# Linear attention with a gated convolution block: key projections in plain float32, plain float32 for the second batch's queries, and the convolution's middle tap on ScalarE

## The chip, the cores and the metric

The kernel runs on one core of a Trainium2 chip. A core has five engines that each work through their own queue in order: TensorE (matmuls; PE in the profile, its weight loads PEld), VectorE (DVE), ScalarE (ACT), GpSimd (POOL) and SyncE (SP), which issues the transfers here. The metric is the time of one execution on the device in microseconds; lower is better.

## The reference, cut to what matters

```python
def _attn_ref(q, k, v, w_phi):                 # batch 8, 8 heads, 576 tokens, head size 64
    def phi(x):
        proj = np.einsum('bhsd,df->bhsf', x, w_phi)          # 128 features
        proj = proj - np.max(np.abs(proj), axis=-1, keepdims=True)
        return np.concatenate([np.exp(proj), np.exp(-proj)], axis=-1)
    q_p, k_p = (phi(q), phi(k))
    kv = np.einsum('bhsf,bhsd->bhfd', k_p, v)
    z = np.sum(k_p, axis=2)
    num = np.einsum('bhsf,bhfd->bhsd', q_p, kv)
    den = np.einsum('bhsf,bhf->bhs', q_p, z)[..., None] + 1e-06
    return num / den

def _moe_ref(x, w_in, conv_w, w_out):          # x: (8, 576, 512), inner width 1024
    h = np.maximum(x @ w_in, 0.0)
    conv_out = conv_w[0]*h[s-1] + conv_w[1]*h[s] + conv_w[2]*h[s+1]   # per channel
    gate = 1.0 / (1.0 + np.exp(-conv_out))
    return h * gate @ w_out
```

The heads of a batch, side by side, are the rows of x. Everything is float32.

## The kernel before, in words

**Two forms of a matmul.** TensorE takes operands of type float32 (plain form) or float32r, a rounded float32. To keep precision with float32r the kernel splits an operand into a rounded part hi and the rest lo (`split`, L57 to L65: one copy at L60, L62 or L64, one subtraction at L65) and makes three matmuls, hi x hi, hi x lo, lo x hi. The expert block's matmuls (hp at L429, op at L488) all have this split form.

**Units and groups.** Each batch is two units of four heads, u = 2*b + qd, 16 in all. A unit's tokens are worked in five groups: g = 0 holds one block of 128 rows (the last 64 tokens of each head pair), g = 1 to 4 hold two blocks each. So a unit has nine blocks.

**Keys** (`k_process`, L220). A group's keys are loaded, split, and projected (`load_split` L172, `project` L185): the lhsT is 128 rows of keys, the rhs the block-diagonal weight, 256 columns, result kp in PSUM. VectorE takes the largest absolute value (L204) and subtracts it (L206), ScalarE makes both exponentials ke (L236, L237), and TensorE multiplies them with v into kv (L251, L255), always plain float32. GpSimd makes the key's split: kxh at L62, kxl at L65.

**Queries** (`q_process`, L300). Load, split or not, project to qp (L196 plain, L199 to L201 split), maximum and subtraction as before, four transposes tp (L320), both exponentials (L326), then the product with kv, nm. `NQ_F32 = 2` makes the first two units' queries plain at the projection. `NKV_F32 = 2` makes the first two units plain at nm (L348); in the later units g = 0 is plain and g = 1 to 4 are split (L356), for which the exponential qe is split by ScalarE (qh at L60) and VectorE (ql at L65), and kv itself by ScalarE (kvf at L279) and VectorE (kvh at L64, kvl at L65). Unit u's nm is interleaved by hand with the kv products of unit u + 1: `after` chains each instruction behind the last, with one kv product behind two of three split matmuls, or n behind each plain one.

**From attention to the expert block.** ScalarE copies numerator and denominator out of PSUM (L374, L379), the denominators go through small transfers (L377), VectorE adds 1e-6 and takes the reciprocal (L392, L393), four transfers spread it into rr (L397), and VectorE and ScalarE make x and its split (L405, L406, L409).

**The expert block** runs over 16 halves n of 288 tokens. `h_part` (L418) makes eight tiles hp of 12 matmuls, each evicted with a Relu by ScalarE into h (L436). The PSUM pool pm that hp and op use has two buffers. `conv_process` (L441) makes the convolution in one tile c (one buffer): the middle tap c = h * cw on GpSimd (L452), the outer taps added by VectorE (L457), one sigmoid on ScalarE over all eight channels' tiles (L461), the gate's product (L465), and the split into gh (ScalarE) and gl (VectorE). `o_part` (L478) makes four tiles op of 24 matmuls, evicted at L493 and stored. A new half's first tap can be written only when the old half's gl have read c.

**What sets the order.** The Python code runs generators under a small planner: each step has a cost in nanoseconds (`pe`), a pause (`wait`), or conditions (`until`), and the loop at the end takes an attention step or an expert step, so that both end together, with the last halves of the expert block alone. The planner's costs do not depend on the form of a matmul. The instructions then go through a scheduler that simulates their times and places them in each engine's queue by readiness and priority. Expert work starts when all four head pairs of the first batch have their x. The 16 weight tiles come as float64 words and are converted by VectorE, ScalarE and GpSimd (L92 to L120) in the first 130 us or so.

Of the kernel before, what the change touches and what calls it, by code (L numbers as in the profile page):

```python
# [11 lines left out]
AF = mybir.ActivationFunctionType  # L12
ALU = mybir.AluOpType
# [7 lines left out]
TC = 288  # L21
# [7 lines left out]
AHEAD = 300  # L29

NQ_F32 = 2
NKV_F32 = 2


@with_exitstack
def kernel(
# [13 lines left out]
    nc = tc.nc  # L50
# [6 lines left out]
    def split(src, hi, lo, eng_hi, eng_lo):  # L57

        if eng_hi is nc.scalar:
            nc.scalar.activation(out=hi, in_=src, func=AF.Copy)  # L60
        elif eng_hi is nc.gpsimd:
            nc.gpsimd.tensor_scalar(out=hi, in0=src, scalar1=1.0, scalar2=0.0, op0=ALU.mult, op1=ALU.add)  # L62
        else:
            nc.vector.tensor_copy(out=hi, in_=src)  # L64
        eng_lo.tensor_tensor(out=lo, in0=src, in1=hi.bitcast(F32), op=ALU.subtract)  # L65
# [56 lines left out]
    cw = cp.tile([P, 24], F32, name="cw")  # L122
# [7 lines left out]
    cw = cw.rearrange("p (f k) -> p f k", k=3)  # L130
# [25 lines left out]
    def wait(ns):  # L156
        return ("wait", ns * LAT)

    def until(*keys):
        return ("until", [k for k in keys if k is not None])  # L160

    def set_ready(key, ns=0):
        ready[key] = now[0] + ns * LAT
# [5 lines left out]
    def group_columns(g):  # L169
        return (512, 1) if g == 0 else ((g - 1) * 256 + (P if g > 2 else 0), 2)  # L170

    def load_split(src, b, qd, g, kind):  # L172
        c0, n = group_columns(g)
        if kind == "q" and 2 * b + qd < NQ_F32:
            raw = sb.tile([P, n * P], F32, name=f"{kind}r{b}_{qd}_{g}", tag=kind + "xh", bufs=2)
            nc.sync.dma_start(out=raw, in_=src[b, qd, :, c0 : c0 + n * P])
            return n, raw, None
        raw = sb.tile([P, n * P], F32, name=f"{kind}r{b}_{qd}_{g}", tag=kind + "r", bufs=2)
        nc.sync.dma_start(out=raw, in_=src[b, qd, :, c0 : c0 + n * P])
        hi = sb.tile([P, n * P], F32R, name=f"{kind}xh{b}_{qd}_{g}", tag=kind + "xh", bufs=2)  # L180
        lo = sb.tile([P, n * P], F32R, name=f"{kind}xl{b}_{qd}_{g}", tag=kind + "xl", bufs=2)
        split(raw, hi, lo, nc.gpsimd, nc.gpsimd)
        return n, hi, lo
# [36 lines left out]
    def k_process(b, qd, g):  # L220
# [4 lines left out]

        yield until(back("kp", 2), back("kv", 4))
        n, hi, lo = load_split(kT, b, qd, g, "k")
        v0 = 16 if g == 0 else 4 * (g - 1)
        v = sb.tile([P, 4 * VW], F32, name=f"v{b}_{qd}_{g}", tag="v", bufs=4)
# [40 lines left out]
        if g == 4:  # L270
# [4 lines left out]
            for i in range(2):  # L275
                kf = None
                if 2 * b + qd >= NKV_F32:
                    kf = sb.tile([P, 2, 2 * VW], F32, name=f"kvf{b}_{qd}_{i}", tag="kvf", bufs=2)
                    nc.scalar.activation(out=kf, in_=kp[i], func=AF.Copy)  # L279
                hi = sb.tile([P, 2, 2 * VW], F32 if 2 * b + qd < NKV_F32 else F32R, name=f"kvh{b}_{qd}_{i}", tag="kvh", bufs=4)  # L280
                if 2 * b + qd < NKV_F32:
                    nc.scalar.activation(out=hi, in_=kp[i], func=AF.Copy)
# [17 lines left out]
    def q_process(b, qd, g):  # L300
# [4 lines left out]

        yield until(back("qp", 2))
        n, hi, lo = load_split(qT, b, qd, g, "q")
        yield wait(3000)
        yield until(back("tp", 2))
# [8 lines left out]
        for t in range(n):  # L318
            for i in range(2):
                nc.tensor.transpose(out=tp[:, i, t, :], in_=pr[:, 2 * t + i, :], identity=idn)  # L320
        f32 = 2 * b + qd < NKV_F32 or g == 0
        qh = sb.tile([P, 2, 2, n * P], F32 if f32 else F32R, name=f"qh{b}_{qd}_{g}", tag="qh", bufs=2)
# [95 lines left out]
    def h_part(n):  # L418
        b, c = divmod(n, 2)
        yield until(*[("x", b, p, c) for p in range(4)], "w_in")  # L420
        spawn(conv_process(n))
        for f in range(8):
            ps = pm.tile([P, HW], F32, name=f"hp{n}_{f}", tag="m")
            k = 0
            for p in range(4):
                xa, xb = xh[b, p, c], xl[b, p, c]
                wa, wb = win_hi[p][:, f * P : (f + 1) * P], win_lo[p][:, f * P : (f + 1) * P]
                for w_, x_ in ((wa, xa), (wa, xb), (wb, xa)):
                    nc.tensor.matmul(out=ps, lhsT=w_, rhs=x_, start=(k == 0), stop=(k == 11))  # L429
                    k += 1  # L430
                if p % 2 == 1:
                    yield pe(740)
            if 8 * n + f >= NH:
                yield until(("gate", 8 * n + f - NH))
            hs = sb.tile([P, HW], F32, name=f"h{n}_{f}", tag="h", bufs=NH)
            nc.scalar.activation(out=hs, in_=ps, func=AF.Relu)  # L436
            ht[n, f] = hs
            set_ready(("hs", n, f), 500)
        set_ready(("h", n))

    def conv_process(n):  # L441
        c = n % 2
        o = 0 if c == 0 else HW - TC
        for f in range(8):
            yield until(("hs", n, f), ("g4", n - 1) if n > 0 else None)
            if f == 0:
                c4 = sb.tile([P, 8, TC], F32, name=f"c{n}", tag="c", bufs=1)
            hs = ht.pop((n, f))
            ct[n, f] = hs, c4
            cv = c4[:, f, :]  # L450

            nc.gpsimd.tensor_scalar(out=cv, in0=hs[:, o : o + TC], scalar1=cw[:, f, 1:2], scalar2=0.0,  # L452
                                    op0=ALU.mult, op1=ALU.add)
            for j in (0, 2):
                lo = 1 if (c, j) == (0, 0) else 0
                hi = TC - 1 if (c, j) == (1, 2) else TC
                nc.vector.scalar_tensor_tensor(out=cv[:, lo:hi], in0=hs[:, o + j - 1 + lo : o + j - 1 + hi],  # L457
                                               scalar=cw[:, f, j : j + 1], in1=cv[:, lo:hi],
                                               op0=ALU.mult, op1=ALU.add)
        yield wait(2000)  # L460
        nc.scalar.activation(out=c4, in_=c4, func=AF.Sigmoid)  # L461
        for f in range(8):
            set_ready(("gate", 8 * n + f))
            hs, c4 = ct[n, f]
            nc.vector.tensor_tensor(out=c4[:, f, :], in0=c4[:, f, :], in1=hs[:, o : o + TC], op=ALU.mult)  # L465
        yield wait(3000)
        yield until(("o", n - 1) if n > 0 else "w_out")
        for f in range(8):
            hs, c4 = ct.pop((n, f))
            if f % 4 == 0:  # L470
                gh4 = sb.tile([P, 4, TC], F32R, name=f"gh{n}_{f}", tag="gh", bufs=2)
                gl4 = sb.tile([P, 4, TC], F32R, name=f"gl{n}_{f}", tag="gl", bufs=2)
            gt[n, f] = gh4[:, f % 4, :], gl4[:, f % 4, :]
            split(c4[:, f, :], *gt[n, f], nc.scalar, nc.vector)
        set_ready(("g4", n))
        set_ready(("g", n), 3000)
# [81 lines left out]
    while moe is not None or chains or active:  # L558
        while chains and sum(1 for p in active if p[2]) < WINDOW:
            b, x, g, kind = chains.pop(0)  # L560
# [82 lines left out]
```

## Time and profile before

| | |
|---|---|
| median of three runs | 827.91 us |
| those runs | 826.32, 827.91, 1064.72 us |
| the profiled execution | 825.6 us, its span 823.5 us, mean granted TensorE clock 0.989 |
| instructions | 17817 |
| read from HBM, written | 38.13 MB, 9.44 MB |

The span is the time from the first profiled instruction to the last. Busy times are sums of an engine's instructions; matmuls overlap in TensorE's pipeline, so the time that one costs is read from the starts of neighbours and not from its own duration. A row of a group gives line, engine, operation, output and inputs by the program's names, shape and count, then busy time and mean duration, then the engine's idle time ahead of these instructions and what ended it.

### The profile page before, as it was taken

The numbers are of one execution on the slowest core, as the hardware profiler recorded it, in microseconds if no ns is written. First come the engines' busy times: TensorE is split into PE (matmuls) and PEld (weight loads), VectorE is DVE, ScalarE is ACT, GpSimd is POOL, SyncE is SP. The second block draws the span as 40 slices with busy tenths as digits, with TensorE's granted clock in tenths as the row PEclk, the third lists the DMA queues.
The fourth block names the chain that finished last, engine by engine and source line by source line (L and its number), as shares of the span: only waits on it lengthen the run. The fifth ranks groups of instructions, "written<-read, shape, count | busy, mean of one in ns | idle before, by whom it ended". The sixth has DMA issues, their size and how long they took to land.

```text
span 823.5 us, 17817 instructions
## 1 busy us (share of the span) xinstructions
PE 788.0 (96%) x6350; PEld 772.5 (94%) x6350; DVE 645.6 (78%) x1390; ACT 569.5 (69%) x1228; POOL 307.6 (37%) x467
## 2 busy tenths in 40 slices
PE   7778779999999999999999999999999999999998
PEld 6767678999999999999999999999999999999998
DVE  4879999799987769787779878788697878766551
ACT  4598777797788867687586857678576867644332
POOL 4757765444443424414233333424334131111110
PEclk9799989999999999999999999999999999999999
DMA  6544421211211302121121211112021100000001
GB/s 187 157 134 135 135 66 47 67 41 44 70 56 44 93 18 71 27 82 50 46 61 43 69 34 60 47 50 82 15 77 29 56 12 19 13 30 30 23 23 44
DMA packets 56328, 49.18 MB, mean 60 GB/s; under 512 B 15024, under 2 KB 54192, under 8 KB 56240
## 3 DMA queue, kind: packets, MB, share of 16 engines
q1 hardware_dynamic: 56240, 48.05, 20.1%
q8 instruction: 51, 0.84, 0.4%
q14 instruction: 37, 0.30, 0.1%
HBM read 38.13 MB, written 9.44 MB: 58 GB/s over the span
## 4 chain that ended last, share of the span: by engine, by line
PE 74%; DVE 10%; ACT 7%; issue 4%; DMA 3%; POOL 1%; SPq 1%; DVEq 0%; ACTq 0%; POOLq 0%
PE op L488 22%; PE hp L429 21%; PE kv L255 8%; PE nm L356 8%; PE tp L320 3%; PE kp L199 2%; PE nm L348 2%; PE kp L200 2%; PE kp L201 2%; PE qp L199 1%; PE qp L200 1%; PE qp L201 1%; DMA w_r<-in_w_in_dram 1%; PE kv L251 1%; DVE qm L204 1%
## 5 line engine op out<-in xcount | busy, mean ns | idle before, releaser
L457 DVE SCALAR_TENSOR_TENSOR c<-h,cw,c 128x287 f32<-128x287 f32 (+1 forms) x256 | 138.7, 554 | 49.4 <-POOL c L452 47.5
L452 POOL TENSOR_SCALAR c<-h,cw 128x288 f32<-128x288 f32 x128 | 75.0, 588 | 243.6 <-ACT h L436 184.3
L255 PE MATMUL kv<-v,ke 128*128 128x65 f32 x1024 | 159.4, 255 | 1.4 <-ACT ke L236 1.2
L255 PEld LDWEIGHTS kv<-v,ke 128*128 128x128 f32 x1024 | 153.5, 193 | 4.8 <-ACT ke L236 1.8
L429 PE MATMUL hp<-xh,win_hi 128*128 128x290 f32 x512 | 153.2, 300 | 0.6 <-ACT os L493 0.6
L429 PE MATMUL hp<-xl,win_hi 128*128 128x290 f32 x512 | 152.7, 298 | 0.2 <-DVE xl L65 0.2
L488 PE MATMUL op<-gh,wout_hi 128*128 128x288 f32 x512 | 152.2, 298 | 0.0
L429 PE MATMUL hp<-xh,win_lo 128*128 128x290 f32 x512 | 151.9, 297 | 0.0
L488 PE MATMUL op<-gl,wout_hi 128*128 128x288 f32 x512 | 151.4, 296 | 0.0
L488 PE MATMUL op<-gh,wout_lo 128*128 128x288 f32 x512 | 150.9, 295 | 0.0
L436 ACT ACTIVATE h<-hp 128x290 f32<-128x290 f32 x128 | 52.2, 414 | 71.7 <-PE hp L429 71.2
L429 PEld LDWEIGHTS hp<-xh,win_hi 128*128 128x128 f32 x512 | 96.7, 190 | 1.5 <-ACT os L493 1.4
L62 POOL TENSOR_SCALAR kxh<-kr 128x256 fp32r<-128x256 f32 (+1 forms) x80 | 43.8, 547 | 144.1 <-PE kp L200 134.6
L429 PEld LDWEIGHTS hp<-xl,win_hi 128*128 128x128 f32 x512 | 97.0, 189 | 0.6 <-DVE xl L65 0.6
L429 PEld LDWEIGHTS hp<-xh,win_lo 128*128 128x128 f32 x512 | 97.1, 190 | 0.0
L488 PEld LDWEIGHTS op<-gh,wout_lo 128*128 128x128 f32 x512 | 96.4, 188 | 0.0
L488 PEld LDWEIGHTS op<-gl,wout_hi 128*128 128x128 f32 x512 | 96.2, 188 | 0.0
L488 PEld LDWEIGHTS op<-gh,wout_hi 128*128 128x128 f32 x512 | 96.1, 188 | 0.0
L65 DVE TENSOR_TENSOR ql<-qe,qh 128x512 fp32r<-128x512 f32 x112 | 79.9, 732 | 9.9 <-ACT qh L60 9.5
L236 ACT ACTIVATE ke<-ks 128x512 f32<-128x512 f32 (+1 forms) x80 | 46.9, 586 | 39.1 <-DVE ks L206 36.5
L326 ACT ACTIVATE qe<-tp 128x512 f32<-128x512 f32 x112 | 61.2, 595 | 12.2 <-PE tp L320 10.4
L356 PE MATMUL nm<-ql,kvh 128*65 128x256 f32 x224 | 68.4, 308 | 0.3 <-DVE ql L65 0.2
(84 smaller groups left out, 1989.5 us busy)
## 6 DMA issues: line engine op xcount, KB each, us to landing
v<-in_vt_dram SPq DMA_DIRECT2D x80, 130.0 KB
out_dram<-os SPq DMA_DIRECT2D x64, 144.0 KB
qr<-in_qT_dram SPq DMA_DIRECT2D x64, 128.0 KB
kr<-in_kT_dram SPq DMA_DIRECT2D x64, 128.0 KB
w_r<-in_w_in_dram SPq DMA_DIRECT2D x8, 512.0 KB
w_r<-in_w_out_dram SPq DMA_DIRECT2D x8, 512.0 KB
rr<-rc SPq DMA_DIRECT2D x128, 2.2 KB
qr<-in_qT_dram SPq DMA_DIRECT2D x16, 64.0 KB
```

The costliest lines, as they stand in the source:

```text
L62: nc.gpsimd.tensor_scalar(out=hi, in0=src, scalar1=1.0, scalar2=0.0, op0=ALU.mult, op1=ALU.add)
L65: eng_lo.tensor_tensor(out=lo, in0=src, in1=hi.bitcast(F32), op=ALU.subtract)
L199: nc.tensor.matmul(out=o, lhsT=his, rhs=wbd_hi, start=True, stop=False)
L236: nc.scalar.activation(out=e[:, 0], in_=pr, func=AF.Exp)
L255: ins = nc.tensor.matmul(out=kp[i][:, s, p0 : p0 + VW], lhsT=lhsT, rhs=v[:, (2 * t + i) * VW : (2 * t + i + 1) * VW], start=False, stop=(g ...
L326: nc.scalar.activation(out=e, in_=tp.rearrange("p i t s -> p i (t s)"), func=AF.Exp, scale=1.0 - 2.0 * s)
L356: ins = after(ins, lambda: nc.tensor.matmul(out=ps[:, i, o : o + w], lhsT=w_, rhs=x_, start=(k == 0), stop=(k == 5)))
L429: nc.tensor.matmul(out=ps, lhsT=w_, rhs=x_, start=(k == 0), stop=(k == 11))
L436: nc.scalar.activation(out=hs, in_=ps, func=AF.Relu)
L452: nc.gpsimd.tensor_scalar(out=cv, in0=hs[:, o : o + TC], scalar1=cw[:, f, 1:2], scalar2=0.0, op0=ALU.mult, op1=ALU.add)
L457: nc.vector.scalar_tensor_tensor(out=cv[:, lo:hi], in0=hs[:, o + j - 1 + lo : o + j - 1 + hi], scalar=cw[:, f, j : j + 1], in1=cv[:, lo:hi ...
L488: nc.tensor.matmul(out=ps, lhsT=w_, rhs=x_, start=(k == 0), stop=(k == 23))
```

## The change

Three edits. The keys' tiles are loaded as float32 and go into the projection unsplit, for all 16 units (before, only queries of the first two units did); the tile uses the buffers (tag kxh, two of them) that held the rounded part, and the matmul reads it directly. `NKV_F32 = 4` takes the second batch's two units into the plain form of nm: their kv is copied out of PSUM once as float32, and the exponentials are written as float32 without a split. The middle tap becomes a ScalarE activation, a copy scaled by a value per partition.

```diff
 NQ_F32 = 2
-NKV_F32 = 2
+NKV_F32 = 4
...
     def load_split(src, b, qd, g, kind):
         c0, n = group_columns(g)
-        if kind == "q" and 2 * b + qd < NQ_F32:
+        if kind == "k" or 2 * b + qd < NQ_F32:
             raw = sb.tile([P, n * P], F32, name=f"{kind}r{b}_{qd}_{g}", tag=kind + "xh", bufs=2)
             nc.sync.dma_start(out=raw, in_=src[b, qd, :, c0 : c0 + n * P])
             return n, raw, None
...
-            nc.gpsimd.tensor_scalar(out=cv, in0=hs[:, o : o + TC], scalar1=cw[:, f, 1:2], scalar2=0.0,
-                                    op0=ALU.mult, op1=ALU.add)
+            nc.scalar.activation(out=cv, in_=hs[:, o : o + TC], func=AF.Copy, scale=cw[:, f, 1:2])
```

## The prediction

> **What bounds the kernel now.** I read the engine totals first, then a table of stages, and only then single instructions.
>
> ```profile
> PE 788.0 (96%) x6350; PEld 772.5 (94%) x6350; DVE 645.6 (78%) x1390; ACT 569.5 (69%) x1228; POOL 307.6 (37%) x467
> ```
>
> One average hides three stages, so the next view is the busy time of each engine per stage (columns: length, then PE, weight load, DVE, ACT, POOL, granted clock, DMA share, GB/s):
>
> ```profile
> 0.00:60.00 60.00, 45.69 (x293) 40.96 (x294) 41.43 (x76) 37.86 (x78) 34.68 (x47) 0.91 0.53 155
> 60.00:140.00 80.00, 64.88 (x497) 58.54 (x496) 78.45 (x147) 61.94 (x134) 56.61 (x66) 0.96 0.35 104
> 140.00:200.00 60.00, 58.48 (x491) 57.70 (x490) 52.83 (x117) 48.77 (x107) 26.98 (x39) 1.00 0.19 53
> 200.00:700.00 500.00, 499.65 (x4190) 497.52 (x4189) 403.33 (x888) 368.10 (x797) 173.13 (x284) 1.00 0.18 50
> ```
>
> From 200 to 700 us TensorE idles 0.35 us in 500: a microsecond more of TensorE work there is a microsecond more of time, and work taken off VectorE or GpSimd there is worth nothing. From 140 to 200 us it idles 1.5 us, nearly the same case. From 60 to 140 us VectorE is busy 78.45 of 80 us and TensorE idles 15.1: there VectorE sets the pace. In the first 60 us TensorE idles 14.3 us with no engine full. So the change has two prices: its TensorE work counts after 140 us, its VectorE work before.
>
> **What a plain product costs on TensorE.** The trap is in the counts. The source has one plain matmul per 128-token block (two query units of nine blocks are plain now, 18 matmuls), and the profile shows twice as many; the split form shows 144 of each of its three, as the source has them.
>
> ```profile
> L196 PE MATMUL qp<-wbd_f,qr 128*128 128x256 f32 x36 | 10.9, 436 | 9.5 <-DMA wbd_f<-in_wbd_dram 4.9 <-ACT qh L326 3.7 <-PE tp L320 0.9
> L199 PE MATMUL kp<-wbd_hi,kxh 128*128 128x256 f32 x144 | 49.0, 340 | 6.2 <-DVE ks L206 4.0 <-POOL wout_lo L65 2.0 <-ACT num L379 0.2
> L348 PE MATMUL nm<-qh,kvh 128*65 128x256 f32 x64 | 19.5, 386 | 1.6 <-ACT qh L326 1.6
> L356 PE MATMUL nm<-qh,kvh 128*65 128x256 f32 x224 | 63.1, 286 | 0.6 <-ACT qh L60 0.6
> ```
>
> So a plain float32 matmul is issued as two instructions. The mean durations (436, 340, 286 ns) overlap in the pipeline and say nothing of cost; the distance from start to start does. In TensorE's timeline:
>
> ```profile
> 15.36 1.46 PE L196 MATMUL qp<-wbd_f,qr 128*128 128x256 f32 x6
> 16.66 0.27 PE L320 MATMUL tp<-idn,qs 128*128 128x128 f32 x1
> ...
> 231.92 0.28 PE L199 MATMUL kp<-wbd_hi,kxh 128*128 128x256 f32 x1
> ...
> 232.27 0.29 PE L199 MATMUL kp<-wbd_hi,kxh 128*128 128x256 f32 x1
> ```
>
> Six plain instructions take 16.66 - 15.36 = 1.30 us, 0.217 each, so a plain block costs 0.434 us. Three split matmuls, from one L199 to the next, take 0.35 us. **Plain is 0.08 us dearer per block.** Bounds: where a split triple follows plain work, its first start-to-start is 0.20 us, not 0.12 (228.12 to 228.32 below), which would make the old form 0.43 and the difference nothing; and a lone plain block between split ones can add that same 0.08 to its successor, which makes it 0.16. As the plain rows before a switch look shortened by about as much, I take 0.08.
>
> ```profile
> 228.12 0.36 PE L199 MATMUL kp<-wbd_hi,kxh 128*128 128x256 f32 x1
> 228.32 0.28 PE L200 MATMUL kp<-wbd_lo,kxh 128*128 128x256 f32 x1
> ```
>
> The Trainium skill, page "FP8 and Floating Point Precision", section "TensorE Precision Notes", says that true float32 takes four passes through the array. Counted as four split matmuls of 0.35/3 = 0.117 us that would be an estimate of 0.47 us a block; the trace has 0.434, and its row is what I use.
>
> The second half of the change on TensorE is L348 for L356 in the second batch. A step of one projection half with its interleaved key products, plain (57.27 to 58.10: two nm, four kv instructions) and split (230.12 to 230.81: three nm and two rows of two kv between):
>
> ```profile
> 57.27 0.59 PE L348 MATMUL nm<-qh,kvh 128*65 128x256 f32 x2
> 57.70 0.56 PE L255 MATMUL kv<-v,ke 128*128 128x65 f32 x4
> 58.10 0.60 PE L348 MATMUL nm<-qh,kvh 128*65 128x256 f32 x2
> ...
> 230.12 0.31 PE L356 MATMUL nm<-qh,kvl 128*65 128x256 f32 x1
> ...
> 230.81 0.31 PE L356 MATMUL nm<-qh,kvl 128*65 128x256 f32 x1
> ```
>
> 0.83 against 0.69 us, 0.14 dearer. Two units, four groups, four steps: 32 steps, 4.5 us.
>
> **The sum by stage.** GpSimd's split of a key group, which goes, and the reach of the key work and of the expert evictions (a tile's view: ns least/median/most, first and last start):
>
> ```profile
> L65 POOL TENSOR_TENSOR kxl<-kr,kxh 128x256 fp32r<-128x256 f32 (+1 forms) x80 | 59.6, 745 | 8.4 <-PE kp L201 4.0
> L62 POOL TENSOR_SCALAR kxh<-kr 128x256 fp32r<-128x256 f32 (+1 forms) x80 | 43.8, 547 | 144.1 <-PE kp L200 134.6 <-DMA kr<-in_kT_dram 9.4
> ...
> L199 PE MATMUL kp<-wbd_hi,kxh x144: 277/362/775, 7.3 to 660.1; 128*128 128x256 f32 x144
> ...
> L436 ACT ACTIVATE h<-hp x128: 392/413/439, 128.1 to 794.7; 128x290 f32<-128x290 f32 x128
> ```
>
> The key blocks per stage are a third of the kp matmuls (same columns, kp's instructions alone), the second batch's first 32 split products with ql lie half before 140 us and half in the next stage:
>
> ```profile
> 0.00:60.00 60.00, 13.45 (x57) 10.78 (x57) 13.01 (x22) 0.91 0.53 155
> 60.00:140.00 80.00, 10.98 (x60) 8.89 (x60) 13.75 (x22) 0.96 0.35 104
> 140.00:200.00 60.00, 8.17 (x39) 6.01 (x39) 8.88 (x14) 1.00 0.19 53
> 200.00:700.00 500.00, 64.73 (x276) 45.60 (x276) 64.20 (x102) 1.00 0.18 50
> ...
> 60.00:140.00 80.00, 5.29 (x16) 2.41 (x16) 10.30 (x10) 0.96 0.35 104
> 140.00:200.00 60.00, 7.32 (x24) 3.25 (x24) 8.32 (x13) 1.00 0.19 53
> ```
>
> 200 to 700 us: 92 blocks x 0.08 = +7.4 us, nothing to hide it. 140 to 200 us: 13 x 0.08 + 16 x 0.14 = +3.3 us. 0 to 60 us: 19 blocks, +1.5 us, against GpSimd's split (0.547 + 0.745 = 1.3 us) that leaves the way of the first key groups and 14.3 us of idle: taken as 0, between -3 and +3. After 700 us no key is projected: 0.
>
> 60 to 140 us: TensorE's +3.8 us (20 x 0.08 + 16 x 0.14) falls into 15.1 us of idle. VectorE loses these (groups of this stage alone, mean ns behind the count):
>
> ```profile
> L65 DVE TENSOR_TENSOR ql<-qe,qh 128x512 fp32r<-128x512 f32 x10 | 10.6, 1070 | 0.0
> L65 DVE TENSOR_TENSOR kvl<-kvf,kvh 128x260 fp32r<-128x260 f32 x4 | 1.7, 415 | 0.0
> L64 DVE CAST kvh<-kvf 128x260 fp32r<-128x260 f32 x4 | 1.2, 289 | 0.0
> ```
>
> That is 13.5 us off a full engine. TensorE's own 64.9 + 3.8 = 68.7 us is the floor, so the stage can shrink by at most 11.3 us. It cannot get all: ql begins only at 103 us, and SP's queue, the evictions and the key waits stay. I take -4 (0 to -11).
>
> In the Trainium skill, page "SBUF — State Buffer", section "Who interferes with whom", a VectorE instruction with two SBUF inputs contends with a GpSimd one that reads SBUF. The ql row agrees, 1070 ns here beside GpSimd busy 56.6 of 80 us; taking the key splits off GpSimd would then help the front beyond the 13.5 us, but not below TensorE's floor.
>
> **The middle tap** leaves GpSimd for ScalarE. Its rows, and the nearest on ScalarE by shape:
>
> ```profile
> L452 POOL TENSOR_SCALAR c<-h,cw 128x288 f32<-128x288 f32 x128 | 75.0, 588 | 243.6 <-ACT h L436 184.3 <-DVE gl L65 50.4 <-ACT dr L374 5.7
> L60 ACT ACTIVATE gh<-c 128x288 fp32r<-128x288 f32 x128 | 45.6, 433 | 5.3 <-PE op L488 5.2
> L60 ACT ACTIVATE qh<-qe 128x512 fp32r<-128x512 f32 x112 | 65.7, 635 | 0.1
> ```
>
> 128 x 0.433 = 55 us more on ScalarE, less 16 x 0.635 = 10 for the splits of qh: 569.5 becomes 615 us. In the 500 us stage that is 368 of 500 plus some 35, still under 82%; the cover is that idle share and the two PSUM buffers of the expert matmuls. The tap itself stands right behind the eviction of h that it reads, in the same queue. I take +1 us of new TensorE stalls, bounds -1 (VectorE waits less for the tap) and +34 (the second rival). The keys' loads now go straight into the tile that the matmul reads, two buffers instead of two and two; a group's load on SP's queue then waits for the matmul two groups back, and behind it stand v, the denominators and the outputs. With 80 groups over 653 us (7.3 to 660.1), two groups are 16 us, so I take 0 (up to +3 in the crowded front).
>
> Sum: 0 - 4 + 3.3 + 7.4 + 1 = **+7.7 us on the profiled run's 825.6, about 833**; its span is 823.5 us with 2.1 around it. The runs shown have 826.3 and 827.9 besides one far out, so I round down a little for the front: **832 us**, 0.5% above the median.
>
> **Rivals.**
> *The front gives everything back.* TensorE idle in 60 to 140 us falls to nothing (-11.3) and the start loses 3: 825.6 - 14.3 + 10.7 + 1 = 823. For it: VectorE's 98%. Against: ql starts late in that stage.
> *ScalarE stands still for the old tile.* The tap writes the single buffer c, free only when VectorE has finished all eight gl of the half before.
>
> ```profile
> POOL c L452 <- DVE gl L65: 50.4, 5, 18.3
> ...
> 701.98 0.42 ACT L436 ACTIVATE h<-hp 128x290 f32<-128x290 f32 x1
> ...
> 702.85 0.51 POOL L452 TENSOR_SCALAR c<-h,cw 128x288 f32<-128x288 f32 x1 [18.30 <-DVE gl L65]
> ```
>
> On GpSimd nobody queued behind these 50.4 us. On ScalarE the evictions do, and it decides once ScalarE stands longer than the two PSUM buffers cover, 2 x 12 matmuls x 0.13 = 3.2 us. All five waits less that cover: 50.4 - 16 = +34, 866 us, slower. Against: in the longest the eviction ended at 702.40 and the tap began at 702.85, so ScalarE would have stood 0.45 us.
> *TensorE pays in full.* The front gives nothing, TensorE's added 1.5 + 3.8 us there count too, and lone plain blocks cost their neighbours 0.08 in half the cases (+5): 825.6 + 5.3 + 10.7 + 5 + 1 = 848.
> *Plain is not dearer.* The change does less than I price: at a difference of 0 per key block, 825.6 - 4 + 2.2 + 1 = 825.
>
> **Chances.** Forecast (826 to 841) 0.55; front gives all back 0.12; plain not dearer 0.12; full price 0.13; ScalarE stands still 0.08. A measurement of this kernel can tell about 2% from no change, here 811 and 844.5 us. The two cheap cases together give 825.6 - 14.3 + 2.2 + 1 = 814.5; below 811 I leave 0.06, for that with a corner of the bounds; above 844.5 lie most of the full price and of the standing ScalarE and a corner of the forecast, 0.17; within, 0.77. The range for eight in ten, 816 to 847, takes in the cheap cases and most of the full price and leaves out the standing ScalarE.
>
> **What would show it.** TensorE busy near 803 us; L196 with kp, 288 instructions at 0.217 us start to start; L348 with 128x256 at 128, L356 at 192 each; GpSimd near 129 us (307.6 less the taps' 75 and the key splits' 103); ScalarE near 615; VectorE near 631 or less. In the steady stage each batch should take 18 blocks x 0.08 = 1.4 us longer. Wrong if it takes less (plain cheaper than its rows), if TensorE shows waits on h or os in the middle (ScalarE), or if the first expert eviction (128.1 us now) doesn't come earlier (the front).

## The result, and the profile after

The changed kernel takes 834.12 us (median of four runs, 831.43 to 837.46) against 826.32 us (median of three); the ratio is 1.0095, 95% interval 1.0074 to 1.0116. It is about one per cent slower, by 7.8 us; the forecast was 832. Runs in a slower state of the chip are left out here and below (of the kernel before 1064.72 and 854.32 us, and one of 1083.95 us of the kernel that keeps GpSimd's copies). The profiled execution of the changed kernel is its fastest run, 831.43 us with a span of 829.6.

Engine totals of the changed kernel, then its busy time by stage (length, PE, weight load, DVE, ACT, POOL, granted clock, DMA share, GB/s):

```profile
PE 799.7 (96%) x6174; PEld 770.0 (93%) x6174; DVE 611.9 (74%) x1366; ACT 623.2 (75%) x1340; POOL 134.2 (16%) x179
```

```profile
0.00:60.00 60.00, 47.31 (x298) 40.13 (x298) 43.62 (x84) 39.66 (x82) 20.47 (x22) 1.00 0.55 162
60.00:140.00 80.00, 73.06 (x498) 63.56 (x497) 67.36 (x135) 62.43 (x140) 38.44 (x40) 0.96 0.35 101
140.00:200.00 60.00, 57.69 (x444) 54.96 (x444) 46.46 (x109) 50.06 (x104) 7.87 (x14) 1.00 0.17 46
200.00:700.00 500.00, 497.06 (x4011) 487.94 (x4010) 381.18 (x868) 395.95 (x858) 67.41 (x104) 1.00 0.18 50
700.00:829.60 129.60, 124.59 (x931) 123.39 (x930) 73.25 (x175) 75.06 (x160) 0.00 (x0) 1.00 0.08 26
```

The first four rows answer to the four of before. From 60 to 140 us VectorE is no longer full (67.4 us instead of 78.45) and TensorE idles 6.9 us instead of 15.1. From 200 to 700 us TensorE idles 2.9 us instead of 0.35, and ScalarE carries 28 us more. The new waits there, by TensorE's weight loads, longest first, are on evictions of op (L492) and on qh:

```profile
PEld hp L429 <- ACT os L492: 1.7, 5, 0.6
PEld op L487 <- ACT os L492: 1.0, 2, 0.8
PEld nm L356 <- ACT qh L60: 0.7, 1, 0.7
```

The groups that the prediction named, with the tap and the evictions of h as a tile's view gives them (ns least/median/most, first and last start):

```profile
L196 PE MATMUL kp<-wbd_f,kr 128*128 128x256 f32 x288 | 81.4, 390 | 3.2 <-DMA kr<-in_kT_dram 1.9 <-PE kv L255 1.3
L348 PE MATMUL nm<-qh,kvh 128*65 128x256 f32 x128 | 40.2, 398 | 3.1 <-ACT qh L326 3.0
L452 ACT ACTIVATE c<-h,cw 128x288 f32<-128x288 f32 x128 | 67.2, 537 | 2.4 <-DVE gl L65 0.2
...
L436 ACT ACTIVATE h<-hp x128: 387/413/452, 114.6 to 800.4; 128x290 f32<-128x290 f32 x128
```

288 and 128 instructions, as two per plain matmul require. The start-to-start of a plain key block shows in TensorE's timeline: two L196 from 455.30 to the next row at 455.73, 0.43 us, the forecast's 0.434.

```profile
455.30 0.59 PE L196 MATMUL kp<-wbd_f,kr 128*128 128x256 f32 x2
455.73 0.27 PE L320 MATMUL tp<-idn,qs 128*128 128x128 f32 x1
```

The period of a batch in the steady stage shows in one eviction of the numerator, L379, in two batches that lie three apart. Before, it comes at

```profile
351.52 0.77 ACT L379 ACTIVATE num<-nm 64x256 f32<-64x256 f32 x2
...
638.97 0.76 ACT L379 ACTIVATE num<-nm 64x256 f32<-64x256 f32 x2
```

and in the changed kernel at

```profile
349.56 0.76 ACT L379 ACTIVATE num<-nm 64x256 f32<-64x256 f32 x2
...
641.85 0.77 ACT L379 ACTIVATE num<-nm 64x256 f32<-64x256 f32 x2
```

so a batch takes 97.4 us instead of 95.8, 1.6 more; 1.4 was forecast.

**Reading the span as a sum.** A span is TensorE's work at full clock, plus its idle time, plus what it loses at a lower granted clock. The loss is the span times one minus the mean clock, good to a microsecond or two, since the mean covers idle time as well. Of before: idle 823.5 - 788.0 = 35.5, loss 823.5 x 0.011 = 9.1, work 788.0 - 9.1 = 778.9. Of the changed kernel: idle 829.6 - 799.7 = 29.9, loss 829.6 x 0.005 = 4.1, work 795.6. So the span's +6.1 is work +16.7, idle -5.6, clock -5.0. The clocks (core, span, clock), before first:

```profile
core 0: 823.5 us, clock 0.989
```

```profile
core 0: 829.6 us, clock 0.995
```

### The profile page after: what moved, and what is told of

Its sections match the earlier page's. It is cut to its first block, busy times and chain, and to the rows that moved or that the text cites. A ratio compares the mean times of both kernels' runs of the same rounds, so it can differ in the third digit from the quotient of the medians.

```text
span 829.6 us, 17001 instructions
## 1 busy us (share of the span) xinstructions
PE 799.7 (96%) x6174; PEld 770.0 (93%) x6174; DVE 611.9 (74%) x1366; ACT 623.2 (75%) x1340; POOL 134.2 (16%) x179
## 4 chain that ended last, share of the span: by engine, by line
PE 74%; ACT 11%; DVE 7%; DMA 4%; issue 2%; SPq 1%; DVEq 0%; ACTq 0%
PE hp L429 22%; PE op L487 19%; PE kv L255 8%; PE nm L356 7%; PE kp L196 6%; PE tp L320 3%; PE nm L348 3%; PE qp L199 1%; ACT gh L60 1%; DMA w_r<-in_w_in_dram 1%; PE qp L200 1%; PE kv L251 1%; PE qp L201 1%; ACT num L379 1%; ACT ke L237 1%
## 5 line engine op out<-in xcount | busy, mean ns | idle before, releaser
L429 PE MATMUL hp<-xh,win_hi 128*128 128x290 f32 x512 | 155.9, 306 | 3.3 <-ACT os L492 1.7
L456 DVE SCALAR_TENSOR_TENSOR c<-h,cw,c 128x287 f32<-128x287 f32 (+1 forms) x256 | 127.4, 516 | 38.3 <-ACT c L452 36.6
L62 POOL TENSOR_SCALAR qxh<-qr 128x256 fp32r<-128x256 f32 (+1 forms) x70 | 32.1, 465 | 463.8 <-PE qp L200 310.3
L487 PEld LDWEIGHTS op<-gh,wout_lo 128*128 128x128 f32 x512 | 96.4, 188 | 0.0
L65 DVE TENSOR_TENSOR ql<-qe,qh 128x512 fp32r<-128x512 f32 x96 | 67.4, 712 | 23.3 <-ACT qh L60 22.8
L196 PE MATMUL kp<-wbd_f,kr 128*128 128x256 f32 x288 | 81.4, 390 | 3.2 <-DMA kr<-in_kT_dram 1.9
L326 ACT ACTIVATE qe<-tp 128x512 f32<-128x512 f32 x96 | 53.6, 597 | 25.3 <-PE tp L320 24.5
L65 DVE TENSOR_TENSOR gl<-c,gh 128x288 fp32r<-128x288 f32 x128 | 55.0, 480 | 21.8 <-ACT gh L60 21.7
L452 ACT ACTIVATE c<-h,cw 128x288 f32<-128x288 f32 x128 | 67.2, 537 | 2.4 <-DVE gl L65 0.2
```

What stands on the lines that cost most here:

```text
L196: nc.tensor.matmul(out=o, lhsT=his, rhs=wbd_f, start=True, stop=True)
L326: nc.scalar.activation(out=e, in_=tp.rearrange("p i t s -> p i (t s)"), func=AF.Exp, scale=1.0 - 2.0 * s)
L452: nc.scalar.activation(out=cv, in_=hs[:, o : o + TC], func=AF.Copy, scale=cw[:, f, 1:2])
```

## The experiments

The theory: plain matmuls add TensorE work that counts after 140 us, and the front is set by VectorE. Its rivals: GpSimd's copies set the front, the tap on ScalarE makes the loss, or the order of the queues does. The first eight kernels are the three edits alone, in pairs, and two versions with plain keys in four units; all twelve kernels stand in one table behind them, split as above. The kernel before, timed again beside them, had medians of 825.6 to 825.9 us; the ratios are against these.

**Keys alone.**

```diff
-        if kind == "q" and 2 * b + qd < NQ_F32:
+        if kind == "k" or 2 * b + qd < NQ_F32:
```

> Only the keys are projected in plain float32; nm and the middle tap are as before. Theory A (TensorE's added work counts after 140 us, the front is set by VectorE): 105 blocks after 140 us at 0.08 us give +8.4 us, the front gains little because VectorE keeps its work, so +6 to +9 us against before (833 to 836); first expert eviction near 126 us. Rival B (GpSimd's reads slow VectorE in the front): taking the key splits off GpSimd frees the front, first expert eviction near 118 us, TensorE idle before 140 us down from 29.4 to about 22, and the total only about +1 us. Rival C (the tap on ScalarE is what costs): keys alone about 0.

845.68 us, ratio 1.0234 (1.0212 to 1.0256): more than twice the loss of the whole change, which no theory expected. First eviction at 121.5 us, between the two. TensorE's work is near its price (+12.8 us), the rest is idle time (+7.6): four batches have a stall of 2.4 or 3.4 us. TensorE's timeline at one of them, then ScalarE's:

```profile
353.99 0.63 PE L348 MATMUL nm<-qh,kvf 128*65 128x64 f32 x8
358.00 0.33 PE L356 MATMUL nm<-qh,kvh 128*65 128x256 f32 x1 [3.37 <-ACT qh L60]
...
359.47 0.44 PE L488 MATMUL op<-gl,wout_hi 128*128 128x288 f32 x1
359.71 0.44 PE L488 MATMUL op<-gh,wout_lo 128*128 128x288 f32 x1
```

```profile
350.69 2.13 ACT L461 ACTIVATE c<-c 128x2304 f32<-128x2304 f32 x1
...
353.44 1.28 ACT L236 ACT_TABLE_LOAD   x1
354.74 0.63 ACT L236 ACTIVATE ke<-ks 128x512 f32<-128x512 f32 x1
355.28 0.61 ACT L237 ACTIVATE ke<-ks 128x512 f32<-128x512 f32 x1
355.91 0.59 ACT L374 ACTIVATE dr<-nm 1x512 f32<-1x512 f32 x1
356.52 0.76 ACT L379 ACTIVATE num<-nm 64x256 f32<-64x256 f32 x2
357.31 1.15 ACT L60 ACTIVATE qh<-qe 128x512 fp32r<-128x512 f32 x2
```

TensorE stands 3.37 us for qh, and ScalarE is never idle in it: qh stands behind the sigmoid, a table load, another group's exponentials and an eviction. The bracket says who ended the wait; the second fence says why so late. Afterwards the expert matmuls start 0.24 us apart, not 0.13.

**nm alone.**

```diff
-NKV_F32 = 2
+NKV_F32 = 4
```

> Only the second batch's nm is plain; keys stay split, the tap stays on GpSimd. Theory A: VectorE loses 13.5 us in the front, first expert eviction 6 to 10 us earlier than 128, TensorE idle before 140 us down by 4 to 8 us; 16 steps after 140 us at 0.14 us give +2.2 us; total -2 to -6 us. Rival B (front relief comes from GpSimd): eviction stays near 128 us and the total is +2 to +4 us.

826.45 us, ratio 1.0011 (0.9999 to 1.0024), no change. The eviction comes at 122.2 us and the work grows by 3.2, as expected; the total misses the expected gain, because idle and clock together give back only 2.4.

**Tap alone.**

```diff
-            nc.gpsimd.tensor_scalar(out=cv, in0=hs[:, o : o + TC], scalar1=cw[:, f, 1:2], scalar2=0.0,
-                                    op0=ALU.mult, op1=ALU.add)
+            nc.scalar.activation(out=cv, in_=hs[:, o : o + TC], func=AF.Copy, scale=cw[:, f, 1:2])
```

> Only the middle tap moves to ScalarE. Theory A: ScalarE about 625 us busy, TensorE gets waits on os and h in the middle, some 2 to 4 us of idle after 140 us, total +1 to +4 us. Rival C (ScalarE is what costs): +6 us or more, with most of the change's loss in it. If the tap costs nothing at all, 0 within 1 us, and the 2.6 us of new idle after 200 us must come from another edit.

827.72 us, ratio 1.0024 (1.0015 to 1.0034), +2 us. It is not what costs.

**The pairs**: keys and nm (the tap put back), keys and tap (nm put back), nm and tap (the keys put back). The edits are the ones above.

```diff
-            nc.scalar.activation(out=cv, in_=hs[:, o : o + TC], func=AF.Copy, scale=cw[:, f, 1:2])
+            nc.gpsimd.tensor_scalar(out=cv, in0=hs[:, o : o + TC], scalar1=cw[:, f, 1:2], scalar2=0.0,
+                                    op0=ALU.mult, op1=ALU.add)
```

> The change with the tap put back on GpSimd. Theory A: the tap's share of the loss goes, 830 to 833 us, and TensorE's waits on os in the middle with it. Rival C: back to 826 or less. No matter which, GpSimd is busy 75 us more than with the whole change.

848.06 us, ratio 1.0259 (1.0240 to 1.0278): without the tap's edit the change is slower by 14 us more. A miss for every theory.

```diff
-NKV_F32 = 4
+NKV_F32 = 2
```

> The change without plain nm. Theory A: VectorE keeps 13.5 us of work in the front, first expert eviction later than the whole change's 114.6 us by 5 us or more, total 836 to 840 us. Rival B: eviction still near 118 us, total within 2 us of the whole change's 834.

834.27 us, ratio 1.0092 (1.0069 to 1.0115), the whole change's time; the eviction comes at 122.0 us, later as theory A says, but the total is below its range and is the one that rival B gave.

```diff
-        if kind == "k" or 2 * b + qd < NQ_F32:
+        if kind == "q" and 2 * b + qd < NQ_F32:
```

> The change without plain keys. Theory A: no key cost after 140 us (8.4 us), the front still relieved on VectorE: 822 to 828 us, the period per batch back at 95.9 us from 97.4. Rival (the period grows because of ScalarE's extra work, not because of the keys): the period stays near 97 us and the total near 834.

826.91 us, ratio 1.0010 (0.9998 to 1.0022): without plain keys the loss is gone. The loss needs the keys; how large it is depends on the tap.

**Plain keys in the first four units only**, with plain nm, and the tap on either engine.

```diff
-        if kind == "q" and 2 * b + qd < NQ_F32:
+        if 2 * b + qd < (4 if kind == "k" else NQ_F32):
```

> Keys are plain only in the first two batches' units (four of 16), nm is plain in the second batch, the tap stays on GpSimd. This keeps the front's relief and drops the key cost after 200 us (92 blocks, 7.4 us) and the tap. Theory A: 826 - 8 (front idle) + 3.3 (140 to 200 us) or a little more of TensorE work, 819 to 824 us, below both kernels. Rival B expects the same, since GpSimd is relieved too. Rival C expects 826. If plain keys are not dearer after 200 us, this is no better than all keys plain with nm.

827.31 us, ratio 1.0015 (1.0000 to 1.0030). A miss: work +7.2 against -5.8 of idle and clock. The front's relief is paid for by the work that buys it.

> Plain keys in the first four units alone, plain nm in the second batch, tap on ScalarE. Against the same kernel with the tap on GpSimd this prices the tap once more: Theory A +1 to +4 us, 821 to 827 us; period 95.9 us per batch as the keys after 200 us are split. If the tap relieves VectorE (shared reads with GpSimd) more than it loads ScalarE, it is 1 to 2 us faster instead.

829.36 us, ratio 1.0045 (1.0029 to 1.0061), above its range; against the same kernel with the tap on GpSimd it is 2 us more, as theory A has it.

**Plain keys in another order.** With the tap on ScalarE the stall is rare: none over 1.2 us behind 140 us in the changed kernel, one of 1.76 us on qh in that with keys and tap. In the changed kernel ScalarE's queue has the exponentials of that query group and qh together, behind the evictions; with the keys alone qe stands ahead of the sigmoid and qh some 14 us behind qe. To have that order without the tap, only a priority is changed.

```diff
-            nc.scalar.activation(out=e, in_=tp.rearrange("p i t s -> p i (t s)"), func=AF.Exp, scale=1.0 - 2.0 * s)
-            if not f32:
-                split(e, qh[:, s], ql[:, s], nc.scalar, nc.vector)
+            with tc.high_priority(offset=600):
+                nc.scalar.activation(out=e, in_=tp.rearrange("p i t s -> p i (t s)"), func=AF.Exp, scale=1.0 - 2.0 * s)
+                if not f32:
+                    split(e, qh[:, s], ql[:, s], nc.scalar, nc.vector)
```

> Plain keys, tap on GpSimd, as in the kernel with the keys alone (843.2 us span, a stall of 2.4 or 3.4 us in nearly every batch while TensorE waits for qh behind a sigmoid and two table loads on ScalarE). The only edit besides: the queries' exponentials and their split get a higher priority of 600, which changes the order in ScalarE's queue and no instruction. Theory D (those stalls come from the queue order that the scheduler made, not from plain keys as such): the stalls go, the period per batch falls from 101.1 to about 97.4 us and the total to 831 to 836 us, as with the tap on ScalarE. Rival E (with the tap on GpSimd, plain keys stall TensorE in any order): it stays at 840 to 848 us.

826.96 us, ratio 1.0013 (1.0004 to 1.0022): 18.7 us less than with the keys alone, without one instruction less on TensorE, and below the range of either theory. ScalarE at the same place, now with the evictions num (L380) and os (L494) ahead of the table load, and qh right behind its own qe:

```profile
346.32 2.13 ACT L462 ACTIVATE c<-c 128x2304 f32<-128x2304 f32 x1
...
349.36 0.77 ACT L380 ACTIVATE num<-nm 64x256 f32<-64x256 f32 x2
350.15 0.71 ACT L494 ACTIVATE os<-op 128x288 f32<-128x288 f32 x2
350.88 1.28 ACT L236 ACT_TABLE_LOAD   x1
...
353.23 1.07 ACT L327 ACTIVATE qe<-tp 128x512 f32<-128x512 f32 x2
354.19 0.63 ACT L60 ACTIVATE qh<-qe 128x512 fp32r<-128x512 f32 x1
```

But qh does not come earlier here: it starts 7.9 us behind the start of the sigmoid, with the keys alone 6.6 us. What differs is TensorE's own queue. With the keys alone the split nm (L356) stands right behind the eight small nm at 353.99; here 32 expert matmuls stand between the two, and the first qh has been done for 2 us when TensorE asks for it:

```profile
352.15 0.63 PE L349 MATMUL nm<-qh,kvf 128*65 128x64 f32 x8
352.59 0.38 PE L489 MATMUL op<-gh,wout_hi 128*128 128x288 f32 x1
...
356.97 0.36 PE L357 MATMUL nm<-qh,kvh 128*65 128x256 f32 x1
```

So the priority shows that the order makes the stall, and at this place it is TensorE's order more than ScalarE's.

**The control**: the same priority on the kernel before.

> The kernel before with the same priority edit alone, as the control of the run beside it. Theory D: there is no stall to remove, so within 2 us of before (824 to 828 us). If it gains 10 us by itself, the run beside it says nothing about plain keys.

833.42 us, ratio 1.0091 (1.0078 to 1.0104): the same edit makes the kernel before 7.8 us slower, with its work unchanged (-0.2), a miss of the expected 824 to 828. The priority is no gain of its own; it draws another order, which suits plain keys and not split ones. Under this priority plain keys make the kernel 6.5 us faster.

**Plain keys, GpSimd's copies kept.** The split is still made, and nothing reads it.

```diff
         split(raw, hi, lo, nc.gpsimd, nc.gpsimd)
+        if kind == "k":
+            return n, raw, None
         return n, hi, lo
```

> Plain keys in the projection, but GpSimd still makes the split of every key group, which nothing reads; tap on GpSimd. Theory A: plain keys cost TensorE about 12 us of work (144 blocks at 0.08 us) with or without GpSimd's copies, so TensorE's busy time is again near 800 us; the period per batch grows by 1.4 us where no queue stalls. Rival B (the front was set by GpSimd): the first expert eviction is back at 128 us instead of 121.5 with the keys alone. If the queue order happens to stall as with the keys alone, the total is above 840, otherwise 832 to 838.

843.91 us (median of four), ratio 1.0214 (1.0198 to 1.0231), work +10.5. The total is above 840, yet not by the stall that the expectation tied to it: behind 140 us TensorE's longest wait here is 1.1 us. What is missing against the keys alone is the earlier start. First evictions of h, in the order keys alone, nm alone, GpSimd's copies kept:

```profile
L436 ACT ACTIVATE h<-hp x128: 392/413/453, 121.5 to 814.4; 128x290 f32<-128x290 f32 x128
```

```profile
L436 ACT ACTIVATE h<-hp x128: 388/413/465, 122.2 to 795.4; 128x290 f32<-128x290 f32 x128
```

```profile
L438 ACT ACTIVATE h<-hp x128: 391/413/452, 129.4 to 810.1; 128x290 f32<-128x290 f32 x128
```

With the copies kept it is back at 129.4 us (128.1 before). So the keys' share in the front's relief comes from GpSimd's copies, 6.6 us or more, and nm's share is 5.9; singly they make 12.5 of the 13.5 us from 128.1 to 114.6. In five pairs of kernels dropping the copies brings the first eviction forward by 6.6 to 11.1 us, in four pairs plain nm does so by 5.9 to 7.4. That nm's share is VectorE's is the prediction's working; no run isolates it. How GpSimd's copies hold the front back is not settled. One VectorE instruction of the front (60 to 130 us) seems to show it, for before, keys alone, copies kept, and at last for the keys in the other order, without copies:

```profile
L103 DVE SCALAR_TENSOR_TENSOR w_t<-w_t,w_r 128x512 f32<-128x512 int32 x9 | 7.1, 789 | 0.0
```

```profile
L103 DVE SCALAR_TENSOR_TENSOR w_t<-w_t,w_r 128x512 f32<-128x512 int32 x9 | 6.0, 669 | 0.0
```

```profile
L103 DVE SCALAR_TENSOR_TENSOR w_t<-w_t,w_r 128x512 f32<-128x512 int32 x9 | 6.9, 765 | 0.0
```

```profile
L103 DVE SCALAR_TENSOR_TENSOR w_t<-w_t,w_r 128x512 f32<-128x512 int32 x9 | 7.7, 854 | 0.0
```

789, 669 and 765 ns for the same work, but then 854, in a kernel without the copies whose first eviction comes at 120.6 us. So this row does not carry it. VectorE's total does show that the copies cost it time: the same 1390 instructions take 645.6 us before, 632.2 with the keys alone, 632.5 in the other order, and 658.8 with the copies kept. Whether this or GpSimd's own queue, which also works on the weights there, sets the first eviction, no run here separates.

**One unit of nm more instead of two.**

```diff
-NKV_F32 = 2
+NKV_F32 = 3
```

> Keys split, tap on GpSimd, plain nm for one unit more than before (three of 16) instead of two. That unit's nm runs ahead of 140 us, where VectorE is full and TensorE idles, so VectorE loses about 7 us there and TensorE's 16 steps at 0.14 us fall into idle time; the fourth unit's nm, which runs where TensorE is full, stays split. Theory A: 1 to 4 us faster than before, 822 to 825 us, the best of all. If what VectorE gives up in the front does not shorten it, 826 within 1 us.

834.95 us, ratio 1.0107 (1.0088 to 1.0125). A miss by ten microseconds: in the profile, its slowest run, the work grows by 0.3, idle and clock by 11.5, with waits of 2.3 us on qh in two batches. No version beat the kernel before.

**All runs**, in us of the profiled executions (before: 778.9, 35.5, 9.1):

| kernel | work | idle | clock loss | ratio |
|---|---|---|---|---|
| the change | +16.7 | -5.6 | -5.0 | 1.0095 |
| keys | +12.8 | +7.6 | -0.7 | 1.0234 |
| nm | +3.2 | -3.2 | +0.8 | 1.0011 |
| tap | -1.2 | +2.0 | +2.5 | 1.0024 |
| keys, nm | +15.3 | +5.0 | +2.8 | 1.0259 |
| keys, tap | +9.1 | -0.9 | +2.6 | 1.0092 |
| nm, tap | +3.7 | -4.4 | +2.5 | 1.0010 |
| front keys, nm | +7.2 | -3.3 | -2.5 | 1.0015 |
| front keys, nm, tap | +6.0 | -3.8 | +1.7 | 1.0045 |
| keys, other order | +8.7 | -4.1 | -1.7 | 1.0013 |
| other order | -0.2 | +2.6 | +7.6 | 1.0091 |
| keys, copies kept | +10.5 | +1.7 | +3.5 | 1.0214 |
| nm, one unit | +0.3 | +1.4 | +10.1 | 1.0107 |

The ratio is from the timed runs, the split from one profile each (the fastest run of the change and of the copies kept, the slowest of the other order and of nm in one unit), so a row's split can be off from its ratio by some microseconds.

## Why the prediction was right, point by point

**TensorE's work: right.** Forecast +11.5 us for 144 key blocks. Six pairs that differ in the keys alone (keys with before, with nm, with tap, with both, in the other order, and with the copies kept against before) give +12.8, +12.1, +10.3, +13.0, +8.9 and +10.5, mean 11.3. For nm, 4.5 forecast; four pairs give +3.2, +2.5, +4.9, +7.6, mean 4.6. The means agree; single pairs lie up to 3 us off, and some share a kernel. The step that carried this was to count instructions ahead of timing them. The period of a batch agrees too: 1.6 us more where 1.4 was forecast, but 1.1 more than in the kernel with nm and tap (96.4), so a part of the 1.6 is the tap's.

**The front: right in kind, its cause half named.** Idle from 60 to 140 us was to take up 3.8 us of work and give 4 more; it fell by 8.2 us, 7.8 forecast. In that stage nm alone takes 6.2 us off the idle time and the keys alone 3.2. But the sum put it down to VectorE's lost work alone, and half of the earlier start comes from GpSimd's copies, as the copies-kept run shows. The prediction had told of this by the Trainium skill, page "SBUF — State Buffer", section "Who interferes with whom". VectorE's totals agree with it: 645.6 us with the copies, 632.2 without; that this is what holds the front back is not shown. It also fits that VectorE came out at 611.9 us where the prediction had near 631 or less: singly nm takes 12.6 us off it, the keys 13.4 and the tap 8.1, and the last two take no instruction off VectorE.

**The first 60 us: outside its bounds.** Taken as 0, -3 to +3. Idle fell by 1.6 us, and the granted clock there was 1.00 instead of 0.91, worth some 5 us more. Other kernels had clocks of 0.89 to 1.00 in that stage, so one profile cannot say whether the change makes it there. Over the whole span the clock was 0.992 to 0.996 in all four runs of the change; in 63 runs of the kernel before its median was 0.987 and its highest 0.994. So the higher clock goes with the change; why is open. No term of the sum had a clock; TensorE's busy time, 799.7 us where near 803 was expected, is lower for the same reason.

**ScalarE: a size, and a sign of being wrong that came.** The tap takes 537 ns, not 433, so ScalarE stands at 623 us, not 615. New idle after 140 us is 0.8 + 2.6 + 0.8 = 4.2 us by stage where 1 was forecast; the kernel with the tap alone has 3.7 there. The waits on os and h in the middle, which the prediction had named as a sign of being wrong on ScalarE, did come, at a small size: 2.7 us on os from 200 to 700 us, where the kernel before has none on os or h. The rival in which ScalarE stands still for the old tile c did not come: the tap waited 0.2 us in all for gl.

**What the total owed to luck.** The sum gave +7.7 and the timed runs +7.8, but not term by term. In the profiles the work is +16.7 where 16.0 was priced. The idle time fell by 5.6 us where the sum has some 8.3, and a clock gain of 5.0 us that nobody priced made up for it. That these two errors cancel is luck. The step from 833 down to 832 rests on no row, and led away from what was measured. What was not priced either is the order in ScalarE's and TensorE's queues. The same plain keys cost 20.0 us in one order and 1.3 in another, both against the kernel before, by kernels that differ in one priority. The changed kernel happens to be one without the stall. For the keys alone the same working gave 833 to 836 us, and the result was 845.68. Why the scheduler draws this order in one case and that in the other was not settled; that the order, and not plain keys as such, makes the stall is shown by the other-order run.

## What to carry to other kernels

Where TensorE is full, count a change's instructions in the profile (a plain float32 matmul is two here) and price them start to start; over six pairs the mean was 11.3 us where 11.5 was priced, with single pairs from 8.9 to 13.0. Work taken off a full helper engine pays only until the next engine is the limit, and in the front here it paid about what the plain form costs (plain nm alone: no change). And judge an edit in more than one order of the queues: a priority alone moved this kernel by 7.8 us up or 18.7 us down, as much as the largest edit.

## What the runs showed of the hardware

A gap of TensorE can cost more than itself. Keys alone, right behind the stall of 3.37 us and behind one of 2.36 us (the column after POOL's is the granted clock):

```profile
358.00:361.00 3.00, 3.00 (x15) 2.90 (x16) 3.00 (x9) 2.87 (x10) 0.00 (x0) 0.71 0.48 137
361.00:364.00 3.00, 3.00 (x19) 3.00 (x19) 2.02 (x4) 2.73 (x6) 0.00 (x0) 0.72 0.16 51
...
459.40:462.00 2.60, 2.54 (x17) 2.44 (x18) 2.52 (x7) 2.49 (x10) 0.00 (x0) 1.00 0.37 108
```

The longer one is followed by a clock of 0.71, the shorter one is not; this kernel's other two, 3.37 and 2.37 us, go the same way. The Trainium skill, page "TensorE: Matmul & The Clock Gate", part 1 on the clock gate, puts the fall at an idle window of some 3.4 us; these four agree. Two gaps in other kernels do not. With nm in one unit more, a gap of 2.26 us is followed by a clock of 0.65:

```profile
359.14 0.33 PE L356 MATMUL nm<-qh,kvh 128*65 128x256 f32 x1 [2.26 <-ACT qh L60]
```

```profile
359.10:362.00 2.90, 2.86 (x16) 2.86 (x17) 2.85 (x7) 2.77 (x10) 1.26 (x2) 0.65 0.36 101
```

With keys and nm, one of 3.37 us is followed by the full clock:

```profile
562.97 0.33 PE L356 MATMUL nm<-qh,kvh 128*65 128x256 f32 x1 [3.37 <-ACT qh L60]
```

```profile
563.00:566.00 3.00, 3.00 (x21) 2.90 (x22) 3.00 (x9) 2.87 (x10) 0.00 (x0) 1.00 0.48 137
```

So the length of the gap alone does not decide it here, and what else does stays open.

A copy on ScalarE with a scale per partition, float32 to float32, takes 537 ns for 128x288; the plain copy of gh, which also rounds to float32r, takes 433.
